# Two-layer attention and MoE kernel on one core: weaving layer-one units into left-over layer-two units, with one unit fewer in each pair of the third batch

## Chip, cores and metric

The kernel runs on one core of a Trainium2 chip. The metric is the device time of one execution in microseconds (us). Before the change four runs took 317.28, 316.82, 317.18 and 317.05 us, with a median of 317.12 us. The engines have short names below: PE is the matrix engine (TensorE), PEld its weight loads, DVE the vector engine, ACT the scalar engine, POOL the GpSimd engine and SP the engine whose queue issues most of the DMA.

## The reference

Eight batches of eight heads are computed. Each head has 512 local queries, keys and values and 32 global ones, with 64 channels. A local query attends to the 32 global keys and to the local keys at most 32 places away. A global query attends to all 544 keys. The result (8 x 544 tokens of 512 channels, 4352 rows) then passes a two-layer network with a hard-swish between the layers.

```python
s_g = scale * np.matmul(q_g, k_all.transpose(0, 1, 3, 2))
out_g = np.matmul(sm(s_g), v_all)
mask = np.abs(pos[:, None] - pos[None, :]) <= window      # window = 32
s_ll = np.where(mask, s_ll, -1000000000.0)
a_l = sm(np.concatenate([s_lg, s_ll], axis=-1))
out_l = np.matmul(a_l, np.concatenate([v_g, v_l], axis=2))
x = concat(out_g, out_l).transpose(0, 2, 1, 3).reshape(B * S, H * D)
h = x @ w_in                       # 512 -> 2048
g = h * np.clip(h + 3.0, 0.0, 6.0) / 6.0
return g @ w_out                   # 2048 -> 512
```

## The kernel before, in words

**Pairs.** The attention is cut into 32 pairs of heads, numbered p, four to a batch b = p // 4, with m = p % 4 (lines 39 to 40, NM = 4). Batches and pairs are counted from zero, so the third batch is b = 2, with pairs 8 to 11. Batches 0 and 1 are written out by hand (lines 640 to 813). Pairs 8 to 31 run in the loop at line 815.

**One pass of the loop.** For pair p the loop emits, in this order: `feed(p)` (DMA loads, POOL casts and DMA transposes for later pairs), `emit_S2(p + 1)` (scores of the next pair: 16 small matmuls into four PSUM banks, four exponentials on ACT into `E`, and four products with the window mask `mk` on DVE), `emit_SG(p + 1)` (scores of the global queries and their exponentials), `emit_AV(p)` (values: 32 small matmuls into two banks, then on DVE a reciprocal and the normalising product `xn` for each bank), `emit_PG(p)` (global queries times values) and `emit_X(p)` (transpose of `xn` into `xt`). For b < 3 and for the last pair of batch 3, `emit_X` uses PE (four transposes `psX`) and a DVE copy. For the first three pairs of batch 3 and for all later batches it is a DMA transpose on SP's queue (line 428).

**Units.** Between these parts stand four slots `M(n[0])` to `M(n[3])`. `M(n)` takes n closures from the front of the list `units` and emits them. Units are the network's work on a batch, made by `moe_units` when the batch's attention is done (line 846). There are 16 layer-one units, u1(c): four 128x512 matmuls into a bank `psH`, an ACT relu into `t`, and a DVE product into `gt{c}`. There are 16 layer-two units, u2(t, c4): four 128x512 matmuls into a bank `po`, where each group of four units (c4 = 0 to 3) ends one output tile of 128 rows, which is copied out of PSUM by DVE for even t and by ACT for odd t, and stored by a DMA. A layer-one unit thus needs ACT and DVE, and three layer-two units in four need PE alone. The number of units to a pair is set by n at line 826: 6 in batch 2, 7 in batches 3 and 4, 8 afterwards. In the list before, a batch's 16 u1 stand behind all left-over u2 of the batch in front, and its own u2 behind them.

**Left-overs.** At the end of batch 2 one u2 is left, at the end of batch 3 five, and at the end of each later batch nine.

**Order on the engines.** PE, ACT and DVE follow an order that the scheduler makes from the program. SP and POOL are pinned to program order (`pin(*QUEUES)`). All PSUM tiles but `pg` come from one pool of seven banks (`psp`, line 52); a tile whose bank was used by an earlier tile waits until that one has been read. `gt`, `xt` and `mk` are f16, and `gt` and `xt` have two buffers for each index.

**End.** After the loop two more units are emitted (line 848). Then the last 14 units (layer two of the last batch) are set aside, the units of the global tokens are put in front of them, and all is emitted.

```python
n = (1, 1, 2, 2) if b == 2 else (1, 2, 2, 2) if b in (3, 4) else (1, 2, 2, 3)
```

Of the kernel before, what the change touches and what calls it, by code (L numbers as in the profile page):

```python
# [14 lines left out]
def kernel(  # L15
# [14 lines left out]
    B, H, Sl, D = q_l.shape  # L30
# [4 lines left out]
    NC = dff // P  # L35
# [43 lines left out]
    NRUN = 2  # L79
# [90 lines left out]
    def load_g(b0, b1, nm):  # L170
        src = {"kg": k_g, "qg": q_g}[nm]
        t = stage()
        nc.sync.dma_start(
            out=t[:, 0:(b1 - b0) * HH * D].rearrange("p (n d) -> p n d", d=D),
            in_=src[b0:b1].rearrange("b (x y) s d -> (y s) (b x) d", x=HH))
        gst[b0, nm] = t

    def cast_G(b0, b1, nm, eng=nc.vector):
        n = wrk.tile([P, 4 * P], FP16, tag=nm + "n", name=nm + "n", bufs=1)
        nb = b1 - b0  # L180
        (eng.copy if eng is nc.scalar else eng.tensor_copy)(out=n[:, 0:nb * P], in_=gst[b0, nm][:, 0:nb * P])
        gst[b0, nm, "n"] = n
# [22 lines left out]
    def emit_G(b0, b1, nm):  # L205
        emit_Gp(b0, b1, nm)
        for x in range(HH):
            copy_G(b0, b1, nm, x)
# [64 lines left out]
    def wrap_q(p):  # L273
        qT = st[p]["qT"]
        last = [i for i in traced if i.engine == ET.Activation][-1]
        nc.scalar.copy(out=qT[:, 0:W], in_=qT[:, Sl:Sl + W])
        follow([i for i in traced if i.engine == ET.Activation][-1], last)

    def emit_S2(p):
        s = st[p]  # L280
        qT, kT = s["qT"], s["kT"]
        E = s["E"] = wrk.tile([P, 2, 2, Sl], FP16, tag="E", name="E", bufs=3)
        pss = [ps_tile(f"psS{i}") for i in range(4)]
        for ch in range(2):
            for w in (*range(1, NT), 0):
                c0 = w * KW if ch == 0 else ((w - 1) % NT) * KW + D
                for e in range(2):
                    r = slice(e * D, (e + 1) * D)
                    nc.tensor.matmul(out=pss[2 * ch + e][:, w * P:(w + 1) * P],  # L289
                                     lhsT=kT[r, c0:c0 + P], rhs=qT[r, w * P:(w + 1) * P])  # L290
        for ch in range(2):
            for e in range(2):
                nc.scalar.activation(out=E[:, ch, e], in_=pss[2 * ch + e], func=EXP,  # L293
                                     scale=qk_scale)
            for e in range(2):
                nc.vector.tensor_tensor(out=E[:, ch, e], in0=E[:, ch, e],  # L296
                                        in1=mk[:, ch].rearrange("p w c -> p (w c)"), op=mult)
# [43 lines left out]
    def emit_SG(p):  # L341
        b, m = divmod(p, NM)
        kT = st[p]["kT"]
        Eg = Egs[p % NE]
        ps = ps_tile("psSG")
        qz = qgz[:, m, b].rearrange("p e s -> p (e s)")
        for u in range(NT + 1):
            c0 = u * KW if u < NT else D
            nc.tensor.matmul(out=ps[:, u * 2 * Sg:(u + 1) * 2 * Sg], lhsT=kT[:, c0:c0 + P], rhs=qz)  # L349
        nc.scalar.activation(out=Eg[:, 0:NT].rearrange("p u e s -> p (u e s)"),  # L350
                             in_=ps[:, 0:NT * 2 * Sg], func=EXP, scale=qk_scale)
        r = slice(D, D + Sg)
        nc.scalar.activation(out=Eg[r, NT].rearrange("p e s -> p (e s)"),
                             in_=ps[r, NT * 2 * Sg:(NT + 1) * 2 * Sg], func=EXP, scale=qk_scale)
        if b >= NRUN:
            sum_E(p)

    xts = {}
# [62 lines left out]
    def emit_den(b):  # L421
        nc.tensor.matmul(out=pgs[b][:, 1].rearrange("p m e s -> p (m e s)"), lhsT=ones,
                         rhs=Ess[b].rearrange("p m e s -> p (m e s)"), skip_group_check=True)
# [18 lines left out]
    def emit_XG(b):  # L442
        pg = pgs[b]
        Lg = wrk.tile([P, NM, Sg], FP32, tag="Lg", name="Lg", bufs=1)
        Rg = wrk.tile([P, NM, Sg], FP32, tag="Rg", name="Rg", bufs=1)
        for e in range(2):
            r = slice(e * D, (e + 1) * D)
            nc.scalar.activation(out=Lg[r], in_=pg[r, 1, :, e], func=LN)
        nc.scalar.activation(out=Rg, in_=Lg, func=EXP, scale=-1.0)
        for e in range(2):  # L450
            r = slice(e * D, (e + 1) * D)
            nc.vector.tensor_tensor(out=xg[r, :, b], in0=Rg[r], in1=pg[r, 0, :, e], op=mult)
# [59 lines left out]
    units = []  # L512

    def M(n):
        for _ in range(n):
            if units:
                units.pop(0)()

    def local_dests(b):
        d = []  # L520
        for t in range(NT):
            row = b * S + Sg
            if t == 0:
                d.append([(W, P - W, row), (0, W, row + Sl - W)])
            else:
                d.append([(0, P, row + t * P - W)])
        return d
# [233 lines left out]
    def feed(p):  # L761
        b, m = divmod(p, NM)
        if p == 15:
            kglob(4, nc.vector)
        if m == 1 and b + 1 < B and b != 3:
            kglob(b + 1, nc.gpsimd)
        if p + 4 < NPAIR:
            if m == 0:
                vglob(b + 1, nc.gpsimd)
                vgsum(b + 1, nc.gpsimd)  # L770
            cast(p + 4, "kqv", nc.gpsimd)
            vshift(p + 4, nc.gpsimd)
        if m == 2 and b + 2 < B:
            load_vg(b + 2)
        if 2 * NM <= p + 3 < NPAIR:
            emit_TD(p + 3)
        if p + 5 < NPAIR:
            load(p + 5)
# [36 lines left out]
    for p in range(2 * NM, NPAIR):  # L815
        b, m = divmod(p, NM)
        feed(p)
        if p == 10:
            load_g(4, B, "kg")
            load_g(4, B, "qg")  # L820
        if p == 12:
            cast_G(4, B, "kg", nc.gpsimd)
            cast_G(4, B, "qg", nc.gpsimd)
        if p == 14:
            emit_G(4, B, "kg")
        n = (1, 1, 2, 2) if b == 2 else (1, 2, 2, 2) if b in (3, 4) else (1, 2, 2, 3)
        M(n[0])
        if m == 0 and b > NRUN:
            emit_den(b - 1)
            emit_XG(b - 1)  # L830
        if p + 1 < NPAIR:
            emit_S2(p + 1)
        M(n[1])
        if p + 1 < NPAIR:
            emit_SG(p + 1)
        if p + 2 < NPAIR:
            wrap_q(p + 2)
        M(n[2])
        emit_AV(p)
        emit_PG(p)  # L840
        M(n[3])
        if p == 14:
            emit_G(4, B, "qg")
        emit_X(p)
        if m == NM - 1:
            units += moe_units(lambda mm, b=b: xts[b][mm], Sl, local_dests(b), last=(b == B - 1))
        pin(*QUEUES)
    M(2)
    emit_den(B - 1)
# [39 lines left out]
```

## Time and profile before

| | |
|---|---|
| median of four runs | 317.12 us |
| profiled execution, its own time | 317.28 us |
| span from first to last instruction in it | 315.5 us |
| PE busy | 305.1 us |
| DVE, ACT, POOL busy | 212.4, 201.7, 150.7 us |
| TensorE clock granted | 1.000 |

The page of the profile gives busy times, shares of the span and instruction counts, and then the span in 40 slices, where a digit is the busy share in tenths. Two groups of matmuls carry most of the time. A row names the line, the engine, the operation, the tile written and those read, the count, the busy time with the mean of one in ns, and the idle time of the engine ahead of these instructions.

```profile
L485 PE MATMUL po<-wout,gt 128*128 128x512 f16 x528 | 122.6, 379 | 0.0
L464 PE MATMUL psH<-xt,win 128*128 128x512 f16 x512 | 119.4, 379 | 2.1 <-DVE gt L476 1.6
```

A row of a timeline has the start in us from the span's start, the length from the first start to the last end of the merged instructions, the engine, the line, the tiles, and in brackets the idle time ahead with what ended it.

### The profile page before, as it was taken

To read this page: it belongs to the slowest core of one execution; us is meant where nothing else is said; L and a number is where in the kernel's file an instruction comes from. 1 tells how busy PE (TensorE), PEld (TensorE's weight loads), DVE (VectorE), ACT (ScalarE), POOL (GpSimd) and SP (SyncE) were. 2 spreads that over 40 slices of the span, in tenths; PEclk is the share of its full clock that TensorE was granted. 3 is DMA by queue.
4 is the path that set the end of the run, shared out by engine and by line. 5 is a ranking of instruction groups with operands and counts; after the bars stand their busy time and mean duration, and the time that the engine had idled before them with its cause. 6 is when DMAs were issued, how large, how long until landed. Compare 5 with 4: busy or idle time off the path is not lost.

```text
span 315.5 us, 7303 instructions
## 1 busy us (share of the span) xinstructions
PE 305.1 (97%) x2704; PEld 162.7 (52%) x2704; DVE 212.4 (67%) x478; ACT 201.7 (64%) x418; POOL 150.7 (48%) x274
## 2 busy tenths in 40 slices
PE   7888999999999999999999999999999999999995
PEld 5454554545555455555555554555555554448444
DVE  5765878897665999579945895468743972479101
ACT  6878676896445984479844993589556941579000
POOL 4889795498766746773676458533411000000000
PEclk9999999999999999999999999999999999999999
DMA  7999999999999899799998998988632002100131
GB/s 218 245 250 250 217 190 165 206 200 173 242 208 233 193 180 175 150 230 177 173 158 192 208 177 176 173 194 162 103 98 85 18 19 83 66 2 1 40 95 68
DMA packets 140260, 48.85 MB, mean 155 GB/s; under 512 B 127552, under 2 KB 136000, under 8 KB 140224
## 3 DMA queue, kind: packets, MB, share of 16 engines
q1 hardware_dynamic: 133440, 43.93, 69.0%
q0 software_dynamic: 6784, 4.46, 10.9%
q8 instruction: 21, 0.34, 0.5%
q14 instruction: 15, 0.12, 0.1%
HBM read 35.13 MB, written 8.91 MB: 140 GB/s over the span
## 4 chain that ended last, share of the span: by engine, by line
PE 79%; DVE 7%; DMA 4%; ACT 4%; issue 2%; POOL 2%; SPq 1%; POOLq 0%
PE po L485 36%; PE psH L464 30%; PE psS L289 3%; DVE gt L476 3%; DMA win<-in_moe_w_in_dram 3%; PE pav L375 2%; PE pav L378 2%; DMA stg<-in_q_l_dram 2%; ACT t L472 1%; DVE E L296 1%; DVE xn L383 1%; PE psSG L349 1%; PE po L497 1%; PE pg L415 1%; ACT E L293 1%
## 5 line engine op out<-in xcount | busy, mean ns | idle before, releaser
L485 PE MATMUL po<-wout,gt 128*128 128x512 f16 x528 | 122.6, 379 | 0.0
L464 PE MATMUL psH<-xt,win 128*128 128x512 f16 x512 | 119.4, 379 | 2.1 <-DVE gt L476 1.6
L476 DVE SCALAR_TENSOR_TENSOR gt<-t,psH 128x512 f16<-128x512 f32 (+1 forms) x144 | 90.0, 652 | 21.1 <-ACT t L472 19.8
L472 ACT ACTIVATE t<-psH,half_col 128x512 f32<-128x512 f32 (+1 forms) x144 | 92.1, 669 | 18.4 <-PE psH L464 16.8
L464 PEld LDWEIGHTS <-win 128*128 128x128 f16 x576 | 53.3, 98 | 53.6 <-issue 1.5
L485 PEld LDWEIGHTS <-gt 128*128 128x128 f16 x528 | 48.4, 98 | 52.2
L296 DVE TENSOR_TENSOR E<-E,mk 128x512 f16<-128x512 f16 x96 | 51.8, 576 | 30.5 <-ACT E L293 29.2
L293 ACT ACTIVATE E<-psS 128x512 f16<-128x512 f32 x96 | 49.8, 604 | 13.8 <-PE psS L289 13.7
L489 ACT COPY ot<-po 128x512 f32<-128x512 f32 x16 | 9.4, 586 | 58.7 <-PE po L485 46.2
L140 POOL CAST kn<-stg 128x512 f16<-128x512 f32 x31 | 19.4, 625 | 36.4 <-DMA stg<-in_k_l_dram 35.9
L401 POOL TENSOR_TENSOR s<-Eg 128x128 f32<-128x128 f16 x24 | 10.7, 444 | 35.4 <-ACT Eg L350 34.6
L489 DVE COPY ot<-po 128x512 f32<-128x512 f32 x17 | 11.7, 690 | 22.6 <-PE po L485 22.1
L383 DVE TENSOR_TENSOR xn<-pav,rc 128x256 f16<-128x256 f32 x64 | 26.1, 421 | 1.3
L140 POOL CAST qn<-stg 128x512 f16<-128x512 f32 x31 | 20.3, 656 | 11.7 <-DMA stg<-in_q_l_dram 11.7
L140 POOL CAST vt<-stg 128x512 f16<-128x512 f32 x32 | 21.2, 663 | 8.9 <-DMA stg<-in_v_l_dram 8.3
L144 POOL COPY vb<-vt 64x512 f16<-64x512 f16 x32 | 20.6, 642 | 2.1
L378 PE MATMUL pav<-vb,E 128*128 128x65 f16 x256 | 19.9, 195 | 0.8 <-DVE vb L223 0.8
L375 PE MATMUL pav<-vt,E 128*128 128x65 f16 x256 | 20.2, 194 | 0.0
L375 PEld LDWEIGHTS <-E 128*128 128x128 f16 x256 | 17.8, 99 | 4.3 <-issue 0.8
L327 ACT ACTIVATE E<-psS 128x512 f16<-128x512 f32 x32 | 16.8, 601 | 4.0 <-PE psS L318 4.0
L378 PEld LDWEIGHTS <-E 128*128 128x128 f16 x256 | 16.9, 97 | 3.0
L289 PEld LDWEIGHTS <-kT 64*128 64x128 f16 x384 | 10.8, 94 | 9.8 <-issue 8.6
(94 smaller groups left out, 272.8 us busy)
## 6 DMA issues: line engine op xcount, KB each, us to landing
stg<-in_k_l_dram SPq DMA_DIRECT2D x32, 256.0 KB, 3.5
stg<-in_q_l_dram SPq DMA_DIRECT2D x32, 256.0 KB, 4.2
stg<-in_v_l_dram SPq DMA_DIRECT2D x32, 256.0 KB, 4.8
out_dram<-ot SPq DMA_DIRECT2D x23, 256.0 KB, 3.9
win<-in_moe_w_in_dram POOLq DMA_DIRECT2D x16, 128.0 KB, 6.6
wout<-in_moe_w_out_dram POOLq DMA_DIRECT2D x16, 128.0 KB, 4.5
out_dram<-ot SPq DMA_DIRECT2D x8, 192.0 KB, 3.1
out_dram<-ot SPq DMA_DIRECT2D x16, 64.0 KB, 2.0
```

What stands on the lines that cost most here:

```text
L140: eng.tensor_copy(out=o, in_=s[c + "f"])
L144: eng.tensor_copy(out=vbs[b % NV][0:D, :, m, vc], in_=vts[b % NV][D:P, :, m, vc])
L293: nc.scalar.activation(out=E[:, ch, e], in_=pss[2 * ch + e], func=EXP, scale=qk_scale)
L296: nc.vector.tensor_tensor(out=E[:, ch, e], in0=E[:, ch, e], in1=mk[:, ch].rearrange("p w c -> p (w c)"), op=mult)
L375: nc.tensor.matmul(out=o, lhsT=E[:, 0, e, w * P:(w + 1) * P], rhs=vt[:, w, m, c], start=True, stop=False, skip_group_check=True)
L378: nc.tensor.matmul(out=o, lhsT=E[:, 1, e, w * P:(w + 1) * P], rhs=vb[:, (w - 1) % NT, m, c], start=False, stop=True, skip_group_check=True)
L383: nc.vector.tensor_tensor(out=xn[:, 2 * w2:2 * w2 + 2].rearrange("p w (e d) -> p w e d", e=2), in0=po[:, :, 1:1 + P].rearrange("p w (e d) ...
L464: nc.tensor.matmul(out=ps[:, 0:n], lhsT=w_in_t[m][:, c * P:(c + 1) * P], rhs=rhs(m), start=(m == 0), stop=(m == NM - 1), skip_group_check= ...
L472: nc.scalar.activation(out=ts[c][:, 0:n], in_=ph[c][:, 0:n], func=RELU, bias=half_col, scale=1.0 / 6.0)
L476: nc.vector.scalar_tensor_tensor(out=gts[c][:, 0:n], in0=ts[c][:, 0:n], scalar=1.0, in1=ph[c][:, 0:n], op0=amin, op1=mult)
L485: nc.tensor.matmul(out=po[t][:, 0:dm], lhsT=gts[c][:, t * P:(t + 1) * P], rhs=w_out_t[c // 4][:, c % 4], start=(c == 0), stop=(c == NC - 1))
L489: (nc.scalar.copy if t % 2 else nc.vector.tensor_copy)(out=ot, in_=po[t][:, 0:dm])
```

## The change

A new function `weave` takes the place of `units += ...` at the end of each batch in the loop. It splits the new batch's list into its 16 u1 and the rest, and empties `units`. The left-over units are cut into a front part of `len(left) % 4` units (four more where `wait` is true, which is for b > 2) and quads of four, so a quad is one whole output tile. The front part goes first. Then the 16 u1 are dealt into one group more than there are quads, and groups and quads alternate, beginning with a group. The rest, the batch's own u2, follows. The second edit lowers the third slot of the pairs of batch 2 from two units to one.

```diff
+    def weave(new, wait):
+        u1s, rest = new[:NC], new[NC:]
+        left, out_ = units[:], []
+        del units[:]
+        h = len(left) % 4 + (4 if wait else 0)
+        out_ += left[:h]
+        quads = [left[i:i + 4] for i in range(h, len(left), 4)]
+        k = len(quads) + 1
+        for g in range(k):
+            out_ += u1s[NC * g // k:NC * (g + 1) // k]
+            if g < len(quads):
+                out_ += quads[g]
+        units.extend(out_ + rest)
...
-        n = (1, 1, 2, 2) if b == 2 else (1, 2, 2, 2) if b in (3, 4) else (1, 2, 2, 3)
+        n = (1, 1, 1, 2) if b == 2 else (1, 2, 2, 2) if b in (3, 4) else (1, 2, 2, 3)
...
         if m == NM - 1:
-            units += moe_units(lambda mm, b=b: xts[b][mm], Sl, local_dests(b), last=(b == B - 1))
+            weave(moe_units(lambda mm, b=b: xts[b][mm], Sl, local_dests(b), last=(b == B - 1)),
+                  b > NRUN)
```

The lists that follow from it: at the end of batch 2 five units are left (one and a quad), so its u1 come as eight, a quad, eight. At the end of batch 3 nine are left: five go first, and then eight u1, a quad, eight u1. At the end of batches 4 to 7 thirteen are left: five go first, and then five u1, a quad, five u1, a quad, six u1.

## The prediction

> **What bounds the kernel now.** I read the page's first two parts, then the waits of TensorE (PE) alone from 50 us on, then the engines' busy time by stretch, and last the timelines of PE, VectorE (DVE) and GpSimd (POOL) where the first two pointed.
>
> ```profile
> PE 305.1 (97%) x2704; PEld 162.7 (52%) x2704; DVE 212.4 (67%) x478; ACT 201.7 (64%) x418; POOL 150.7 (48%) x274
> PE   7888999999999999999999999999999999999995
> ```
> ```profile
> PE psH L464 <- DVE gt L476: 1.2, 4, 0.4
> ```
>
> PE is the bound, and after the head it waits for one thing only: a PSUM bank for a layer-one unit that DVE's `gt` product has not yet emptied. The starts of its matmuls tell more than these waits. In a full stream two 128x512 matmuls start 0.216 us apart (101.50 to 103.24 for eight), so a unit of four takes 0.865 us.
>
> ```profile
> 100.95 0.62 PE L289 MATMUL psS<-qT,kT 64*128 64x128 f16 x16
> 101.50 1.90 PE L464 MATMUL psH<-xt,win 128*128 128x512 f16 x8
> ...
> 106.32 2.75 PE L464 MATMUL psH<-xt,win 128*128 128x512 f16 x12 [0.41 <-DVE gt L476]
> 109.01 0.62 PE L289 MATMUL psS<-qT,kT 64*128 64x128 f16 x16
> 109.78 1.89 PE L464 MATMUL psH<-xt,win 128*128 128x512 f16 x8 [0.15 <-DVE gt L476]
> ...
> 117.06 0.81 PE L289 MATMUL psS<-qT,kT 64*128 64x128 f16 x16
> 118.28 1.97 PE L464 MATMUL psH<-xt,win 128*128 128x512 f16 x8 [0.41 <-DVE gt L476]
> ```
>
> A score block and its successor normally start 0.55 us apart (100.95 to 101.50). By such distances the starts lost are: 0.57 before 106.32 (the matmul ahead started at 105.72 and takes 0.03), 0.22 at 109.78, 0.15 at 114.16, 0.67 between 117.06 and 118.28, 0.07 after it, then 0.26 at 149.09 and 0.15 at 153.47. That is 2.1 us, all of it in the pairs of batches three and four (batches are counted from zero, and stretches named by the batch whose attention runs), and nothing after 154 us. This is the whole stock that the weave can win. The engines behind it:
>
> ```profile
> 100.00:120.00 20.00, 19.03 (x174) 9.77 (x172) 17.45 (x38) 17.65 (x37) 11.35 (x20) 1.00 0.95 187
> 120.00:138.00 18.00, 18.00 (x181) 9.74 (x179) 13.56 (x33) 9.10 (x24) 12.31 (x20) 1.00 0.86 170
> ```
>
> The columns after the length are PE, weight loads, DVE, ACT, POOL. With layer-one units in every slot DVE and ACT are 87% and 88% busy; with layer-two units ACT falls to 51%.
>
> **What the Trainium skill says.** "Perfetto Trace Analysis", Identifying the Most-Contended Engine, calls matmul busy time a bad measure because matmuls are pipelined. The trace agrees: one lasts 379 ns in the table of groups yet the next starts 216 ns later, so I count starts. "TensorE: Matmul & The Clock Gate", Wait — 56ns, not 53.3ns?, gives 215.7 ns for 512 columns warm, so nothing but waits can be won here. "SBUF — State Buffer", SBUF: two separate sides, says that a DVE operation with two SBUF inputs and a GpSimd operation lock each other out of a shared port pair for a whole instruction. The mask product `E*mk` has two such inputs, and its tile's view gives it 426 ns at the median and 1228 ns at most. The Optimization Strategy section of the first page suggests interleaving regimes with different bounds, which is what the weave does.
>
> **The change, part by part.** No operation is added or removed: 528 + 512 large matmuls stay, so the time can move only by PE's waits. The instruction order is the same up to the batch-two pairs (some 75 us).
>
> *Five units per pair in batch two.* One 0.865 us unit goes from between the score block S2(p+1) and the value block AV(p), four times, 3.46 us of work moved later and not saved. What it covered is the chain S2, ACT's exponentials, DVE's masks, reciprocals and normalised `xn`, PE's transposes psX, which stand behind two more units after AV.
>
> ```profile
> 74.60 3.47 DVE L296 TENSOR_TENSOR E<-E,mk 128x512 f16<-128x512 f16 x4 [1.57 <-ACT E L293]
> ...
> 78.75 0.42 DVE L383 TENSOR_TENSOR xn<-pav,rc 128x256 f16<-128x256 f32 x1
> ...
> 81.38 2.44 DVE L296 TENSOR_TENSOR E<-E,mk 128x512 f16<-128x512 f16 x4 [1.27 <-ACT E L293]
> ```
> ```profile
> 73.38 0.62 PE L289 MATMUL psS<-qT,kT 64*128 64x128 f16 x16
> ...
> 79.04 0.47 PE L436 MATMUL psX<-ident,xn 128*128 128x128 f16 x4
> ```
> ```profile
> 73.67 1.88 POOL L147 COPY vb<-vg 32x2048 f16<-32x2048 f16 x1
> ```
>
> S2 to psX is 5.66 us in each of the four pairs (73.38 to 79.04, 80.31 to 85.97). It becomes 4.80; the second half of `xn` is wanted 0.11 later, at 4.91.
> - Pair 8: the masks run beside POOL's copy of the global values and take 3.47 instead of 2.4. They end 4.69 after S2, and `xn` at 79.17, 5.79 after it. psX already waits (0.47; those of the next pairs take 0.39). S2 starts at the same time in both kernels, so psX ends at the same time too: the whole 0.86 is lost.
> - Pairs 9 and 11: masks end 3.51 and 3.47 after S2, normalising takes 1.1 more, `xn` is there at 4.6. Margin 0.3: no loss, 0.3 each if POOL sits less well.
> - Pair 10: in the changed order the output copy `ot` (0.6 of DVE's time, the queue moves on that fast) stands between the masks and the reciprocals. 3.67 + 0.6 + 0.9 to 1.1 is 5.2 to 5.4: loss 0.25 to 0.5, and I take 0.3.
>
> Sum 1.15, between 0.9 (pair 8 alone) and 2.1. Banks for AV are no problem: it takes those of the first two scores, read 1.6 us after S2, and comes at 2.5. The key and query transposes on SP's queue land over 7 us ahead of their scores (issued 80.85, used from 94.0), and scores come about 2.4 us sooner; no loss. POOL stands idle for its loads in these pairs, and PE's sum of exponentials waits on POOL's results with a pair in hand.
>
> *The weave in batch three* (batch two's u1 run there). `left` is 5 units at that end, h is 1, so there is one quad and the sequence is u2, eight u1, four u2, eight u1. The first eight u1 are those of before, in the same slots: six in pair 12, two in pair 13. The waits at 106.32 and 109.78 (0.79) are these, so the weave does not reach them. What differs is that slot p12.0 now ends output tile 2, copied by DVE in idle time, instead of tile 3, copied by ACT (0.59) just ahead of the logarithms. DVE's `xg` and masks end 0.5 sooner, so the fifth unit finds its bank. But the eighth wants the fifth's bank, whose `gt` stands behind relus after ACT's 2 us of exponentials and both `xn`: about 8.5 after S2, wanted at 8.1. I leave 0.45 there, between 0.2 and 0.8. Then the quad gives DVE 3.5 us with no product, and the 0.15 + 0.67 + 0.07 go. The second eight meet the `kgT` copies (four, 0.28 each) in pair 14: 0.1, between 0 and 0.3.
>
> *The weave from batch four on.* `wait` adds four u2, so `left` 9 gives h = 5, and 13 gives 5 again. The first new u1 comes in slot p16.3, where it stood already; in batches five to seven it comes five units earlier than before. It needs the last `xt`, a DMA transpose that lands 2.4 to 5.6 us after issue by its tile's view. From `xn` to its use lie five to eight units and one score block, over 6 us: no loss. The 0.26 and 0.15 belong to the eleventh and fifteenth unit of a run of sixteen, which is now cut in two: 0.05 left, at most 0.2. From batch five on there was no wait and there is nothing to win. The end of the kernel keeps its order (global tokens, then the last batch's layer two); only the 16 u1 ahead of it are spread.
>
> Sum: 2.1 lost before; after 1.15 + 0.45 + 0.1 + 0.05 = 1.75. Gain 0.35 us. The profiled execution took 317.28 us with a span of 315.5 (1.8 outside it), and stands 0.16 above the median; 317.12 - 0.35 is 316.8.
>
> **The rivals.**
> - *Nearly even* (forecast), 316.8, own range 316.2 to 317.3: the stalls in batch three and those made in batch two pay each other.
> - *The weave wins*: the head of batch three loses only its low end 0.2, pair 10 fits, pair 8 loses 0.86. 2.1 - 1.1 is 1.0: 316.1. For it: DVE starts batch three 0.5 sooner. Against: in pair 13 the bank waits for a product late in DVE's queue.
> - *Slower: the short pairs bind on the mask chain.* Place: psX in pairs 9 to 11. Price: if POOL collides there as in pair 8, masks end 4.69 after S2, `xn` 5.8, and psX loses 0.9 each; 0.86 + 2.7 + 0.6 against 2.1 is 2.1 slower, 319.2; half of it gives 318. It decides when the three lose over 0.5 each, which is masks ending 4.2 after S2. Against: those pairs showed 3.5 to 3.7, though POOL was casting then too.
> - *Loads fall behind*: scores in batch three wait for their transposes; 7 us of margin must go first. About 318.
> - *The change does not act where it means to* is true of the first eight units of both batches and is in the forecast.
>
> **How the numbers follow.** Nearly even 0.52, weave wins 0.27, mask chain 0.16, loads 0.05. A measurement here tells 0.2% (0.63 us) from no change. Of the forecast's own spread 0.09 lies beyond that on the fast side and 0.01 on the slow one. Faster 0.27 + 0.09 = 0.36, slower 0.16 + 0.05 + 0.01 = 0.22, within 0.42. The low end 315.9 takes in the weave's win with pair 14 and batch four at zero; the high end 318.0 takes half the mask case. Outside lie less than 2 in 10.
>
> **What would show it.** psX of pair 8 should wait about 0.9 us for `xn` and end within 0.1 us of 79.4; psX of pair 10 about 0.3; none in pairs 9 and 11. At S2 of pair 13's scores PE should be 2.0 to 2.4 us ahead of before, with 3.46 us of work still owed. One wait for `gt` should remain near the eighth u1 of batch three and none from there to the end. I am wrong if psX waits in all four pairs, if several `gt` waits remain after the quad, or if u1 waits for `xt`.

## The result and the profile after

| | before | after |
|---|---|---|
| median | 317.09 us (54 runs) | 318.42 us (34 runs) |
| lowest and highest | 315.66, 319.21 us | 316.13, 319.99 us |
| profiled execution, its own time | 317.28 us | 317.56 us |
| span of it | 315.5 us | 315.8 us |

The ratio after to before is 1.0039, with a 95% interval from 1.0028 to 1.005, so the changed kernel is slower by 0.39%. The medians stand 1.33 us apart, the means 1.24 us. Four executions in a slower state, three of the kernel before (324 us and more) and one of the version in the last row of the experiments' table (320.31 us), are left out of medians and ratios. The forecast was 316.8 us in a range of 315.9 to 318.0, so the measured median lies above the range. One profiled execution shows less than the medians do, 0.28 us, because it is one draw from a wide spread. For this reason six executions of the changed kernel and two of the old one were traced in all.

The first rows of the page after, and the waits of PE from 50 us on:

```profile
PE 305.3 (97%) x2704; PEld 162.9 (52%) x2704; DVE 220.0 (70%) x478; ACT 202.6 (64%) x418; POOL 151.6 (48%) x274
PE   8898999998999999999999999999999999999995
```
```profile
PE psX L436 <- DVE xn L383: 1.3, 2, 1.1
PE psH L464 <- DVE gt L476: 0.7, 1, 0.7
```

PE is as busy as it was, but DVE grew from 212.4 to 220.0 us with the same 478 instructions, so its instructions took longer each (212.4 and 214.0 us in two traces before, 217.1 to 220.0 in six after). PE now waits for two things instead of one. The first is new: the transposes of pair 8 wait for the normalised values. Here are both on PE's timeline after, with the score blocks of pairs 9, 11, 13, 14 and 16 around them:

```profile
72.75 0.62 PE L289 MATMUL psS<-qT,kT 64*128 64x128 f16 x16
...
78.79 0.28 PE L436 MATMUL psX<-ident,xn 128*128 128x128 f16 x2 [1.08 <-DVE xn L383]
79.33 0.28 PE L436 MATMUL psX<-ident,xn 128*128 128x128 f16 x2 [0.26 <-DVE xn L383]
...
85.21 0.39 PE L436 MATMUL psX<-ident,xn 128*128 128x128 f16 x4
...
86.39 0.62 PE L289 MATMUL psS<-qT,kT 64*128 64x128 f16 x16
...
91.19 0.39 PE L436 MATMUL psX<-ident,xn 128*128 128x128 f16 x4
...
97.17 0.39 PE L436 MATMUL psX<-ident,xn 128*128 128x128 f16 x4
...
98.46 0.62 PE L289 MATMUL psS<-qT,kT 64*128 64x128 f16 x16
...
104.12 2.75 PE L464 MATMUL psH<-xt,win 128*128 128x512 f16 x12 [0.70 <-DVE gt L476]
106.81 0.62 PE L289 MATMUL psS<-qT,kT 64*128 64x128 f16 x16
107.46 1.02 PE L464 MATMUL psH<-xt,win 128*128 128x512 f16 x4
...
122.33 0.93 PE L289 MATMUL psS<-qT,kT 64*128 64x128 f16 x16
```

From the scores to the transposes there are now 4.80 us (86.39 to 91.19), as computed. Pairs 9 to 11 don't wait. Pair 13's scores start at 98.46, 2.49 us ahead of before; pair 8 began 0.63 us sooner in this execution, and in the mean of six the lead is 2.25 us, within the 2.0 to 2.4 of the forecast. The first score block in the fence, at 72.75, leads to a wait of 1.08 us and one of 0.26 in pair 8. Batch three begins with one wait for `gt`, at 104.12, and has no more. The block at 122.33 takes 0.93 where it should take 0.62: its second half starts late.

On DVE's timeline after, the rows behind these waits are the mask products of pairs 9 to 13 (as scores are made one pair ahead, the product at 73.97 belongs to pair 9 and stands ahead of the normalising of pair 8):

```profile
73.97 4.21 DVE L296 TENSOR_TENSOR E<-E,mk 128x512 f16<-128x512 f16 x4 [1.33 <-ACT E L293]
...
81.47 2.26 DVE L296 TENSOR_TENSOR E<-E,mk 128x512 f16<-128x512 f16 x4 [1.27 <-ACT E L293]
...
87.45 2.04 DVE L296 TENSOR_TENSOR E<-E,mk 128x512 f16<-128x512 f16 x4 [1.39 <-ACT E L293]
...
93.43 2.15 DVE L296 TENSOR_TENSOR E<-E,mk 128x512 f16<-128x512 f16 x4 [1.40 <-ACT E L293]
...
100.11 3.24 DVE L296 TENSOR_TENSOR E<-E,mk 128x512 f16<-128x512 f16 x4
103.38 1.88 DVE L476 SCALAR_TENSOR_TENSOR gt<-t,psH 128x512 f16<-128x512 f32 x3
```

And POOL's timeline after, where the global values of the next batch are copied once in four pairs:

```profile
73.77 1.89 POOL L147 COPY vb<-vg 32x2048 f16<-32x2048 f16 x1
...
99.77 1.89 POOL L147 COPY vb<-vg 32x2048 f16<-32x2048 f16 x1
```

Four masks take 2.0 to 2.3 us, except twice: 4.21 and 3.24 us. Both times the copy lies upon them. The second meeting is new. Here are POOL's and DVE's timelines before at that place (two views):

```profile
98.60 1.88 POOL L147 COPY vb<-vg 32x2048 f16<-32x2048 f16 x1
```
```profile
102.68 0.43 DVE L296 TENSOR_TENSOR E<-E,mk 128x512 f16<-128x512 f16 x1 [2.17 <-ACT E L293]
...
103.63 1.92 DVE L296 TENSOR_TENSOR E<-E,mk 128x512 f16<-128x512 f16 x3
```

The copy ran from 98.60 to 100.48 and the masks began at 102.68. After the change the masks begin at 100.11, because PE is 2.5 us ahead, while the copy ends at 101.66: POOL waits for its loads, and its copy even came 1.2 us later.

The tile view of `E` after, between 72 and 82 us, gives shortest, median and longest ns of its mask products:

```profile
L296 DVE TENSOR_TENSOR E<-E,mk x6: 814/825/1965, 71.8 to 81.5; 128x512 f16<-128x512 f16 x6
```

The longest is 1965 ns, where the kernel before had 1228 at most. Beside the 0.43 us that a product took at the median before, it was held for 1.5 us, which is most of the 1.69 us for which the copy still ran when the masks began. The link holds in all twenty traces of the study: from 66 us on they have 1940 mask products, 36 of which took over 1.0 us, and the copy lay upon each of the 36; the longest of the others took 0.88 us.

By stretch (the columns are length, PE, weight loads, DVE, ACT, POOL, clock, DMA share, GB/s):

```profile
100.00:120.00 20.00, 19.27 (x186) 10.30 (x184) 17.86 (x39) 16.47 (x36) 12.10 (x20) 1.00 1.09 195
120.00:138.00 18.00, 17.90 (x162) 9.20 (x161) 14.32 (x34) 10.11 (x23) 12.57 (x21) 1.00 1.04 186
```

In the first stretch, which now holds work that stood some 2.5 us later before, PE gained 0.24 us, and ACT is eased, 16.47 us for 17.65, as the weave spreads the layer-one units; DVE is not, 17.86 for 17.45.

**Bookkeeping.** From pair 8's scores to the last matmul, the time less the late matmul starts is 240.1 to 240.3 us in the traces of both kernels. So the late starts and the time at which pair 8 begins account for an execution. They add up as follows, in us. The mean of six executions of the changed kernel is over traces with times from 317.18 to 319.40 us; the two before took 317.28 and 317.2. The count takes nothing off where the matmuls behind a wait start closer together than usual, so it runs some 0.1 us high where a score block is interrupted, and up to 0.4 us in a whole trace.

| late starts at | before (two traces) | after (this trace) | after (mean of six) | prediction |
|---|---|---|---|---|
| transposes of pair 8 | 0.08, 0.49 | 1.66 | 1.40 (1.15 to 1.78) | 0.86 more than before |
| transposes of pairs 9 to 11 | 0 | 0 | 0.03 | 0.3 |
| first eight layer-one units of batch three | 0.80, 0.86 | 0.97 | 1.32 (0.68 to 2.68) | 0.45 |
| rest of batch three, to pair 16's scores | 0.89, 0.89 | 0.31 | 0.31 | 0.1 |
| batch four | 0.39, 0.24 | 0.09 | under 0.1 | 0.05 |
| all, with those too small to list | 2.28, 2.64 | 3.19 | 3.28 | 1.75 |

Pair 8 begins at 68.97 us in the mean of six and at 68.91 in the mean of two, so nothing is lost ahead of it. The mean of the times is 318.08 against 317.24, which is 0.84 more; that of the late starts 3.28 against 2.46, which is 0.82 more. The traces thus explain 0.84 us of the 1.33 between the medians (1.24 between the means); six draws from a spread of 4 us leave room for the rest.

### The profile page after: what moved, and what is told of

The parts are those of the page before. It is cut to its first block, busy times and chain, and to the rows that moved or that the text cites. A ratio compares the mean times of both kernels' runs of the same rounds, so it can differ in the third digit from the quotient of the medians.

```text
span 315.8 us, 7301 instructions
## 1 busy us (share of the span) xinstructions
PE 305.3 (97%) x2704; PEld 162.9 (52%) x2704; DVE 220.0 (70%) x478; ACT 202.6 (64%) x418; POOL 151.6 (48%) x274
## 4 chain that ended last, share of the span: by engine, by line
PE 86%; DVE 9%; ACT 3%; issue 1%; ACTq 0%
PE po L485 35%; PE psH L464 33%; PE psS L289 4%; DVE E L296 2%; PE pav L375 2%; PE pav L378 2%; DVE gt L476 2%; DVE xn L383 2%; PE psSG L349 1%; PE psS L302 1%; PE psS L318 1%; PE warm L570 1%; PE po L497 1%; PE pg L415 1%; ACT E L327 1%
## 5 line engine op out<-in xcount | busy, mean ns | idle before, releaser
L485 PE MATMUL po<-wout,gt 128*128 128x512 f16 x528 | 124.2, 379 | 0.0
L476 DVE SCALAR_TENSOR_TENSOR gt<-t,psH 128x512 f16<-128x512 f32 (+1 forms) x144 | 91.9, 655 | 37.1 <-ACT t L472 35.8
L472 ACT ACTIVATE t<-psH,half_col 128x512 f32<-128x512 f32 (+1 forms) x144 | 93.1, 670 | 34.8 <-PE psH L464 33.7
L296 DVE TENSOR_TENSOR E<-E,mk 128x512 f16<-128x512 f16 x96 | 55.2, 617 | 9.1 <-ACT E L293 7.9
```

The lines of the kernel that those rows point to most:

```text
L296: nc.vector.tensor_tensor(out=E[:, ch, e], in0=E[:, ch, e], in1=mk[:, ch].rearrange("p w c -> p (w c)"), op=mult)
L472: nc.scalar.activation(out=ts[c][:, 0:n], in_=ph[c][:, 0:n], func=RELU, bias=half_col, scale=1.0 / 6.0)
L476: nc.vector.scalar_tensor_tensor(out=gts[c][:, 0:n], in0=ts[c][:, 0:n], scalar=1.0, in1=ph[c][:, 0:n], op0=amin, op1=mult)
L485: nc.tensor.matmul(out=po[t][:, 0:dm], lhsT=gts[c][:, t * P:(t + 1) * P], rhs=w_out_t[c // 4][:, c % 4], start=(c == 0), stop=(c == NC - 1))
```

## The experiments

Ratios are against the kernel before on the same chip, with 95% intervals; a ratio need not be the quotient of the medians (1.0034 for the version with the unit kept in pairs 9 to 11, whose median is 0.19% above that of before). "Late starts" are counted in the one trace of each kernel, from pair 8 on.

| kernel | median, us (runs) | ratio, interval | traced time; late starts |
|---|---|---|---|
| changed, copy moved behind the casts | 318.38 (22) | 1.0033, 1.0017 to 1.0049 | 316.03; 1.19. Second trace 319.47; 4.10 |
| before, copy moved likewise | 317.26 (14) | 1.0012, 0.9995 to 1.0029 | 316.82; 2.55 |
| changed, fifth unit kept ahead of the values | 317.27 (14) | 1.0006, 0.9989 to 1.0023 | 317.50; 1.97 |
| before, five units per pair, no weave | 317.71 (22) | 1.0019, 1.0004 to 1.0033 | 318.44; 2.85 |
| changed, no copy in the loop | 317.43 (22) | 1.0013, 0.9999 to 1.0027 | 316.94; 2.42 |
| before, no copy in the loop | 316.77 (14) | 0.9987, 0.9968 to 1.0007 | 317.09; 1.35 |
| unit kept and copy moved | 317.76 (22) | 1.0014, 0.9996 to 1.0032 | 317.74; 2.21 |
| unit kept and copy cut in four | 317.89 (22) | 1.0037, 1.0016 to 1.0057 | 319.76; 5.40 |
| unit kept in pair 8 alone | 318.04 (14) | 1.0029, 1.0006 to 1.0052 | 317.41; 1.48 |
| unit kept in pairs 9 to 11 alone | 317.80 (22) | 1.0034, 1.0016 to 1.0051 | 317.39; 2.63 |
| unit kept, five layer-two units first | 316.98 (21) | 1.0005, 0.9985 to 1.0025 | 316.17; 1.44 |

### The copy moved behind the casts

The edit moves the copy of the global values (`vglob`), and the shorter second copy of them (`vgsum`, which despite its name makes no sums), behind the casts in POOL's program order, in the changed kernel and, as a control, in the kernel before.

```diff
         if p + 4 < NPAIR:
+            cast(p + 4, "kqv", nc.gpsimd)
+            vshift(p + 4, nc.gpsimd)
             if m == 0:
                 vglob(b + 1, nc.gpsimd)
                 vgsum(b + 1, nc.gpsimd)
-            cast(p + 4, "kqv", nc.gpsimd)
-            vshift(p + 4, nc.gpsimd)
```

> The changed kernel with one edit: POOL copies the global values of the next batch behind the four casts and shifts of a batch's first pair instead of ahead of them; every other engine keeps its order. Theory A (the loss is the meeting of this 1.9 us copy with the mask products): the four masks of pair 8 fall from 4.2 to about 2.3 us, the psX wait of pair 8 from 1.6 to at most 0.2, the gt wait at the head of batch three from 0.9 to about 0.4, and the time by 1.5 to 2 us, to 0.998 of before or less. Theory B (the short pairs alone, whatever POOL does): psX of pair 8 still waits about 0.9 and the time stays within 0.3 us of the changed kernel.

> The kernel of before with the same move of POOL's copy as in the run named late. In before the copy lies on pair 8's masks (3.5 us) but six units hide them, and it ends ahead of batch three's masks. Theory A expects a change under 0.3 us either way: psX of pair 8 loses its 0.08, the gt waits of batches three and four stay at about 2 us. A theory that POOL's copy costs time in itself expects a gain of 1 us here too.

The median did not move: 318.38 against 318.42. The trace, with 316.03 us the shortest of any changed kernel, looked as if the cure had worked. Its tile view of `E` in the same stretch:

```profile
L296 DVE TENSOR_TENSOR E<-E,mk x10: 410/474/801, 71.6 to 81.9; 128x512 f16<-128x512 f16 x10
```

With the copy at 77.80, no product took over 801 ns, pair 8 did not wait, and the late starts came to 1.19. As trace and median contradicted each other, the same kernel was traced again.

> The kernel of the run named late again (POOL's copy behind the casts). Its profiled execution took 316.03, the shortest of its 22, and lost only 1.2 us from pair 8 on, with a median of 318.38. Theory C expects psX waits in pairs 9 to 11 where this execution is longer than 317.5; theory D psH waits for xt in batches five to seven; theory E a later start of pair 8's scores than 69.1 us.

This time 319.47 us. POOL's copy came at 81.47, on the masks of the pair behind. DVE's and PE's timelines of that trace:

```profile
75.10 1.89 DVE L296 TENSOR_TENSOR E<-E,mk 128x512 f16<-128x512 f16 x4 [1.70 <-ACT E L293]
80.92 4.11 DVE L296 TENSOR_TENSOR E<-E,mk 128x512 f16<-128x512 f16 x4 [1.02 <-ACT E L293]
```
```profile
85.65 0.28 PE L436 MATMUL psX<-ident,xn 128*128 128x128 f16 x2 [0.82 <-DVE xn L383]
86.19 0.28 PE L436 MATMUL psX<-ident,xn 128*128 128x128 f16 x2 [0.26 <-DVE xn L383]
```

The wait of pair 8 has become one of pair 9: 1.41 us of late starts. So for the transposes the mechanism stands: masks without the copy take 1.9 to 2.0 us and masks with it 4.1, and in none of the twenty traces do the transposes `psX` lose over 0.1 us without it. Batch three lost 2.47 more, and about 2.0 of that has another cause: its first eight layer-one units were late between 107 and 110 us, although the masks of pair 13 took 1.89 us, with no copy near them (it came at 110.12). What they waited for is shown further down, where the changed kernel is traced again. The theory that a later copy would win 1.5 to 2 us falls: POOL's order fixes only what the copy stands behind, and its time varies by 3.7 us between two executions of one kernel. In the kernel before, the move changed nothing that the interval tells from zero.

### The fifth unit kept between scores and values

The change takes a unit out of the third slot, ahead of the values. Here the five units per pair stay, but the empty slot is the first one, ahead of the next pair's scores.

```diff
-        n = (1, 1, 1, 2) if b == 2 else (1, 2, 2, 2) if b in (3, 4) else (1, 2, 2, 3)
+        n = (0, 1, 2, 2) if b == 2 else (1, 2, 2, 2) if b in (3, 4) else (1, 2, 2, 3)
```

> The changed kernel with the missing unit of batch two's pairs taken ahead of the scores (0, 1, 2, 2) and not between scores and values. The score block and the transposes stand 5.66 us apart again. Theories A and B both expect the psX wait of pair 8 to go (0.5 at most where the masks still meet POOL's copy, since they then end about 4.8 us after the scores) and a gain of 1.1 to 1.6 us over the changed kernel. Theory A expects the gt wait at the head of batch three to stay at 0.6 to 1.0; a theory that the loss sits in the weave itself expects no gain.

The scores to the transposes are 5.66 us again, pair 8 loses 0.39 in the trace, and the median is 317.27, 1.15 us below the changed kernel and level with before. Everything else of the change, the weave and the number of units, is the same. So the place from which the unit is taken costs about 1.1 us, most of the loss; by the two intervals it can be anything from 0.2 to 2 us.

### The short pairs without the weave

```diff
-        n = (1, 1, 2, 2) if b == 2 else (1, 2, 2, 2) if b in (3, 4) else (1, 2, 2, 3)
+        n = (1, 1, 1, 2) if b == 2 else (1, 2, 2, 2) if b in (3, 4) else (1, 2, 2, 3)
```

This is the only edit, made in the kernel before.

> The kernel of before with five units per pair in batch two and no weave; five layer-two units then stand ahead of batch two's layer-one units. If the short pairs make the loss, the psX wait of pair 8 is 0.9 to 1.6 us, and about four gt waits come back in batches three and four (1 to 2 us), so that it is 1 to 2 us slower than before. If the weave makes the loss, it is within 0.3 us of before.

The loss is 0.19% (0.6 us, less than the 1 to 2 us expected), half of the whole change's, with 1.41 us late at pair 8. The weave on top of it did not win its 1.3 us. Batch three's first rows on PE's timeline tell why:

```profile
99.40 0.62 PE L289 MATMUL psS<-qT,kT 64*128 64x128 f16 x16
99.95 1.90 PE L485 MATMUL po<-wout,gt 128*128 128x512 f16 x8
101.84 1.89 PE L485 MATMUL po<-wout,gt 128*128 128x512 f16 x8
104.20 2.75 PE L464 MATMUL psH<-xt,win 128*128 128x512 f16 x12
```

Without the weave, all five left-over layer-two units come first. They need no bank that waits for DVE, so the masks beside the copy (3.54 us at 101.06) hurt nobody, and no start is late at 104.20. The weave puts only one of the five first and eight layer-one units behind it, right under the slow masks. Later on it takes away 1.32 us (0.34, 0.67, 0.07 and 0.24 here) and leaves 0.4; at the start it adds the 1.32 that the six traces show in the mean. By these traces, then, the weave on top of the short pairs loses 0.4 us rather than winning; between the medians it is 0.7.

### The changed kernel traced again

Five more traces of the changed kernel and one more of the kernel before, with no edit.

> The changed kernel again, for one more trace: its 34 runs lie between 316.1 and 320.0 us, and the one profiled so far (317.56) is one of the shorter. Counting lost starts of matmuls from pair 8's scores on, that one lost 3.2 us of 243.5 and the rest, 240.3, is the same in all traces so far to 0.2. Theory C: executions of 318.4 and more lose 4 us or more, as psX waits for xn also in pairs 9 to 11, where the masks meet POOL's casts. Theory D: they lose it in batches five to seven, where the first layer-one units wait for a DMA transpose. Theory E: they lose it ahead of pair 8, where both kernels have the same order.

> As for again1: a further trace of the changed kernel, to see where a longer execution loses its starts. Theories C, D and E as there.

> The changed kernel, a fourth trace. Theory F: in executions over 318.5 the gaps at the head of batch three come so close together that the granted clock falls to a half for some 3 us behind them, as in the trace of the run named slot0_split (0.52 from 107.5 to 111), which adds 1 to 2 us. Theory C (psX in pairs 9 to 11 too) and E (a later start of pair 8) as before.

> The changed kernel, a fifth trace; theories F, C and E as for again3.

> The changed kernel, a sixth trace. The five so far lost 2.7 to 3.2 us from pair 8 on and took 317.2 to 318.6. If it takes over 319, theory F expects a stretch with the granted clock below 0.8, theory C a psX wait in pairs 9 to 11, theory E a start of pair 8's scores later than 70 us.

> The kernel of before again, for a second trace beside its first (2.3 us of lost starts from pair 8's scores on, at 69.1 us): the sum of its lost starts should be 2.0 to 2.6 us again, and the head of batch three 0.6 to 1.0 of it.

They took 318.35, 317.18, 318.64, 317.33 and 319.40 us, and 317.2 for the kernel before. Pair 8 waits in all five, and pairs 9 to 11 lose 0.09 at most, in the short and in the long ones: theory C, that the spread comes from there, falls. Theory D falls as well, as nothing is lost in batches five to seven. That the loss comes from ahead of pair 8 (E) falls too, by the equal means above, although pair 8 begins anywhere from 68.24 to 69.86 us. What differs between executions is, first, how late POOL's copy is. By its second start, at 98.89, 99.58, 99.77, 100.90, 101.09 and 101.49 us in the six, the first units of batch three lost 0.68, 0.90, 0.97, 1.42, 1.27 and 2.68. In the first of these, which is the shortest execution, the masks took 2.28 us; in the last, the longest, 3.43, and PE's timeline there has four waits:

```profile
104.55 2.75 PE L464 MATMUL psH<-xt,win 128*128 128x512 f16 x12 [0.90 <-DVE gt L476]
107.83 0.56 PE L289 MATMUL psS<-qT,kT 64*128 64x128 f16 x8 [0.36 <-DVE gt L476]
108.71 0.39 PE L289 MATMUL psS<-qT,kT 64*128 64x128 f16 x7 [0.32 <-DVE xn L383]
109.30 1.02 PE L464 MATMUL psH<-xt,win 128*128 128x512 f16 x4 [0.19 <-DVE gt L476]
```

That is 2.68 us of late starts. The granted clock was 1.000, so a fall of it (theory F) isn't needed for a long execution.

The masks explain only the first of the four waits: in two other traces they took longer (3.68 and 3.54 us) and half as much was lost. A second thing differs: when the queries of pair 14 arrive. Behind `emit_SG`, each pass of the loop also calls `wrap_q(p + 2)`, in which ACT copies a piece of the transposed queries `qT` of pair p + 2. So ACT needs that DMA transpose about 3 us before PE needs it for the scores (106.00 and 109.01 for pair 14 before). While ACT waits, the relus `t` behind this copy wait too, and with them the products `gt`, which give PE its banks back. These rows are from ACT's timelines before, after and in the longest trace, and from DVE's in the longest:

```profile
106.00 0.22 ACT L276 COPY qT<-qT 128x32 f16<-128x32 f16 x1
```
```profile
103.24 0.22 ACT L276 COPY qT<-qT 128x32 f16<-128x32 f16 x1
```
```profile
105.46 0.22 ACT L276 COPY qT<-qT 128x32 f16<-128x32 f16 x1 [2.01 <-DMA qT<-qn]
```
```profile
106.42 0.69 DVE L476 SCALAR_TENSOR_TENSOR gt<-t,psH 128x512 f16<-128x512 f32 x1 [1.32 <-ACT t L472]
```

Before, the transpose landed at 100.27 us, 5.7 ahead of ACT's copy. In the profile after it landed at 103.07, 0.17 ahead: the copy came 2.8 us sooner, while the transpose was issued 0.9 us later and took 4.4 us instead of 2.5. In the longest trace it landed at 105.43, and ACT stood idle for 2.01 us. Six traces of versions with layer-one units at the head of batch three separate the two causes, as no mask product of pair 13 took over 0.9 us in them. Their late starts, in us, are counted here by whole distances, without the 0.1 that an interrupted score block adds:

| trace | ACT's wait for the queries | first eight layer-one units late by |
|---|---|---|
| copy moved, first trace | 0 | 0.58 |
| changed, 317.18 us | 0 | 0.58 |
| changed, no copy | 0.56 | 1.12 |
| unit kept and copy moved | 0.72 | 1.28 |
| copy moved, second trace | 1.42 | 1.99 |
| unit kept, copy cut in four | 2.03 | 2.64 |

So in these traces ACT's wait is passed on in full. In the trace of the short pairs without the weave ACT waited 1.51 us and PE lost nothing there, as layer-two units stood in its place. ACT waits over 0.5 us here in seven of the sixteen traces with five units per pair, and in none of the four with six. No run moves this copy or the transpose, so what the wait costs in the medians isn't measured.

### Without the copy

The call of the copy is taken out of the loop, in both kernels; which part of the values that leaves out stands in the expectation.

```diff
             if m == 0:
-                vglob(b + 1, nc.gpsimd)
                 vgsum(b + 1, nc.gpsimd)
```

> The changed kernel without POOL's copy of the global values in the loop: batches three to seven keep the global values of an earlier batch in their value tile, so that part of their local outputs is left out. If the meeting of that copy with the mask products is the loss, psX of pair 8 waits 0.2 us or less, lost starts from pair 8 on fall from 3 to about 1 us in the median, and the time to 316.0 to 316.6 us, ratio 0.997 to 0.999, with fewer runs above 318. If the copy is not the cause, the ratio stays at 1.003 to 1.004.

> The kernel of before without that copy (the same part left out). Its pairs of six units hide the copy in batch two, but the gt waits of batches three and four are made by the layer-one units: expected is a gain of 0 to 0.4 us over before, so less than half of what the changed kernel gains from the same cut, and lost starts near 2 us.

The changed kernel gains, from 1.0039 to 1.0013, though less than expected (317.43 us, where 316.0 to 316.6 stood in the expectation). The old one goes from 1 to 0.9987, which its interval doesn't tell from nothing. In the changed kernel's trace no `psX` waits; 1.23 us remain at the head of batch three, where ACT waits 0.56 us for the queries, and a layer-one unit at 165.41 us is 0.56 late, waiting for the DMA transpose of `xt`, as in no other trace. The copy is worth 0.26% (0.8 us) after and 0.13% (0.4 us) before, by ratios whose intervals are 0.2% to 0.4% wide. So it explains a part of the loss, about 0.4 us of it by these values, and not all.

### Combinations

Three versions build on the kept unit: the copy moved, the copy cut into four pieces behind the casts of four pairs, and all five left-over layer-two units put ahead of the layer-one units of batch two.

```diff
             if m == 0:
-                vglob(b + 1, nc.gpsimd)
                 vgsum(b + 1, nc.gpsimd)
             cast(p + 4, "kqv", nc.gpsimd)
             vshift(p + 4, nc.gpsimd)
+            nc.gpsimd.tensor_copy(
+                out=vbs[(b + 1) % NV][rg, :, m, vc],
+                in_=vg[rg, b + 1].rearrange("s (m h) d -> s m (h d)", h=2)[:, m].unsqueeze(1)
+                .to_broadcast([Sg, NT, P]))
...
-                  b > NRUN)
+                  b >= NRUN)
```

> The changed kernel with both edits: the missing unit taken ahead of the scores, and POOL's copy behind the casts. If the two causes add, it is 0.5 to 1 us faster than the kernel with slot 0 alone (317.27), 316.5 or so, ratio 0.998. If the copy's place matters little in the median, as the run named late suggests, it is equal to slot 0 within 0.3 us.

> A full kernel: the changed one with the missing unit taken ahead of the scores (0, 1, 2, 2), and POOL's 1.9 us copy cut into four of about 0.6 us, one behind the casts of each pair. If the meeting of a long copy with the masks is what remains of the loss (0.4 at psX of pair 8, about 1.0 at the head of batch three), lost starts fall from 2.0 to about 1.0 us and the time to 316.2 to 316.6, ratio 0.997 to 0.999. If short POOL work collides as much as one long copy, it stays at 317.3.

> A full kernel: the run named slot0, with all five left-over layer-two units of batch one put ahead of batch two's layer-one units, so that these begin in slot 3 of pair 12, behind the logarithms and the first masks. If the weave of batch two loses because its first six units stand in pair 12 with the logarithms and the global products, the waits near the head of batch three fall from about 1.0 to 0.4 us, a wait of 0.7 comes back near the last units (no quad is left to cut the run of sixteen), batch four keeps its gain, and the time is 316.6 to 317.1, ratio 0.998 to 1.000. If not, it is equal to slot0 or slower.

Moving the copy adds nothing to the kept unit (317.76 against 317.27, intervals overlapping). Cutting it is no better in the median (317.89), although its pieces took only 0.6 to 0.8 us each and no mask product of pairs 9 to 13 took over 0.9 us: in its trace ACT waited 2.03 us for the queries. Putting the layer-two units first did what it should in its trace, the shortest but one of the study. The wait at the head of batch three is gone, although the copy lay on the masks (3.45 us) and ACT waited 1.21 us for the queries:

```profile
101.92 2.75 PE L464 MATMUL psH<-xt,win 128*128 128x512 f16 x12
...
113.67 1.97 PE L464 MATMUL psH<-xt,win 128*128 128x512 f16 x8 [0.41 <-DVE gt L476]
```

Of its 1.44 us of late starts 0.87 lie in the run of sixteen layer-one units, which this order has again, and 0.45 in batch four. Its median, 316.98, is that of the kernel before on the same chip (317.04). No version of the study is clearly faster than before: this one and the kept unit are level with it.

### Which of the short pairs

The unit is kept in pair 8 alone, or in pairs 9 to 11 alone, with the weave.

```diff
+        n = (0, 1, 2, 2) if p == 8 else (1, 1, 1, 2) if b == 2 else (1, 2, 2, 2) if b in (3, 4) else (1, 2, 2, 3)
```
```diff
+        n = (1, 1, 1, 2) if p == 8 else (0, 1, 2, 2) if b == 2 else (1, 2, 2, 2) if b in (3, 4) else (1, 2, 2, 3)
```

> The changed kernel with slots (0, 1, 2, 2) in pair 8 alone; pairs 9 to 11 keep (1, 1, 1, 2). If psX of pair 8 is the place where the short pairs lose, it equals the run named slot0 (1.0006) within 0.3 us, about 1 us faster than the changed kernel. If pairs 9 to 11 lose as well in longer executions, it stays at 1.002 to 1.004.

> The complement of the run named pair8: pair 8 keeps (1, 1, 1, 2) and pairs 9 to 11 have (0, 1, 2, 2). If psX of pair 8 is the one place of the loss, it equals the changed kernel, ratio 1.003 to 1.004, with 1.2 to 1.8 us lost at psX of pair 8. If the short pairs 9 to 11 share it in executions that the traces miss, as the 1.0029 of pair8 suggests, it lies about half way between slot0 and the changed kernel, 1.001 to 1.003.

In the traces the matter is plain: with the unit kept in pair 8 its late starts are 0.39, with it taken there they are 1.41, and pairs 9 to 11 lose nothing in either. In the ratios it is not. A short pair 8 alone gives 1.0034, nearly the whole loss; but keeping the unit in pair 8 alone gives 1.0029, and not the 1.0006 of keeping it in all four. Both intervals hold 1.002 to 1.005, and that of the second reaches down to 1.0006. How much of the loss the pairs 9 to 11 carry stays open.

## Why the prediction was wrong

**Right.** The operations, the distance of 4.80 us, and the claim that time moves only by PE's waits hold. Pair 8 waits, and pairs 9 and 11 don't. In no trace of the changed kernel does PE wait for a transpose of keys or queries, or for `xt`. The weave takes away the late starts of the second part of batch three and those of batch four, down to 0.31 and under 0.1 us. None of the three signs that were to show the forecast wrong came: the loss lay in sizes and places that they did not cover.

**Wrong, pair 8.** "They end 4.69 after S2, and `xn` at 79.17" took the masks' 3.47 us from one execution as if it were their length. It was not: that copy had begun 0.93 us before the masks and had 0.95 us left, and the longest product took 1.23. In the profile after, the copy starts 0.20 us before them, one product takes 1.97, and the masks end 5.43 after S2 (72.75 to 78.18). Pair 8 loses 1.40 us in the mean where 0.86 was added to an old loss that was near nothing: 0.5 too little. The page of the Trainium skill "SBUF — State Buffer", SBUF: two separate sides, on which the step rested, says that whoever comes second waits for the whole instruction; a product held for 1.5 us of the copy's remaining 1.69 agrees, to 0.2 us. The bound to take from it was the copy's full length, and it stood in the text without being used.

**Wrong, the head of batch three.** "DVE's `xg` and masks end 0.5 sooner, so the fifth unit finds its bank", and 0.45 us left of 0.79. The masks took 3.24 us instead of 2.35 (0.43 + 1.92 before), and 1.32 us are lost in the mean. The step moved PE and DVE forward by the units that were taken out, and left out that POOL's copy would not move with them: it ended 2.2 us ahead of the masks before, and lies on them after. This is the larger of the two, 0.87 us, but not all of it is the copy's. By an estimate from the traces it has three parts. About 0.1 us is lost beyond the forecast where neither copy nor wait is at work (0.58 for 0.45). About 0.2 comes from the wait for the queries in the longest trace, which lost some 1.2 us more than two others with masks as long, spread over six. The rest, about 0.5, comes from the copy.

**Wrong, the query transposes.** "The key and query transposes on SP's queue land over 7 us ahead of their scores" is right for pair 14 before (100.27 and 109.01), but the first to need the queries is ACT, in `wrap_q`, 3 us sooner. The 5.7 us that were left there shrank to 0.17 in the profile after, and ACT waited 0.20, 0.25 and 2.01 us in three of the six traces. The step set this at "no loss"; what it cost is within the 0.87 above. The rival that loads fall behind had a late transpose right and the place wrong, the scores; it was given 0.05.

**Wrong, small.** Pair 10 was to lose 0.3 and lost nothing, since its masks took 2.04; pair 16's scores lose 0.3, where 0.1 was left for the stretch.

These terms, 0.54 + 0.87 - 0.3 + 0.2, make up 1.3 of the 1.5 us between 1.75 and 3.28; the rest are starts late by under 0.05. The rival that the short pairs bind on the mask chain had the mechanism, an operation of POOL upon the masks, and a fair price (318 for half of it). It had the place wrong: not pairs 9 to 11, but pair 8 and the start of batch three. It was given 0.16, because the margins of pairs 9 to 11, which do hold, were read as speaking against it as a whole.

**Open.** The traces of six executions explain 0.84 of 1.33 us. Whether longer executions, in the tail up to 319.99, lose in other places or wait oftener for the queries is not known; nor is the share of pairs 9 to 11.

## What to carry to other kernels

When work on one engine is moved ahead, list the long operations of engines that are paced by something else, here POOL by its loads, and ask what they will now lie upon: they don't come along. Do the same for every reader of a transfer, not only for the last one: here the scores had 7 us to spare, while ACT's copy of the same queries ran out of its margin. A chain that runs beside such an operation is to be priced with its full length and not with the overlap that one execution shows. And where a kernel's executions spread by 4 us, one trace is one draw: the shortest trace of a changed kernel here, 316.03 us, came from a version with a median of 318.38.

## What was not expected of the hardware

In the trace of the kept unit with the copy cut in four (319.76 us), TensorE's granted clock fell in the middle of the kernel. Its busy times by stretch; the columns are PE, weight loads, DVE, ACT, POOL, and then the clock:

```profile
100.00:104.00 4.00, 4.00 (x38) 2.12 (x37) 1.93 (x4) 1.95 (x6) 1.05 (x2) 1.00 1.12 97
104.00:107.50 3.50, 1.78 (x19) 0.89 (x18) 2.67 (x7) 3.48 (x8) 1.26 (x3) 1.00 1.29 244
107.50:111.00 3.50, 3.32 (x8) 1.14 (x9) 3.50 (x7) 2.21 (x5) 3.33 (x5) 0.52 1.21 215
111.00:115.00 4.00, 4.00 (x42) 2.25 (x41) 2.11 (x6) 1.19 (x4) 3.74 (x9) 0.99 1.09 230
```

In 3.5 us PE was busy for only 1.78, waiting four times for `gt` and `xn` behind ACT's 2.03 us wait for the queries, and the 3.5 us after that ran at 0.52 of the clock: eight matmuls, each 0.21 us late, 1.7 us in all beside the 2.65 us of waits. The page of the Trainium skill "TensorE: Matmul & The Clock Gate", Part 1: The HAM clock gate (the "warmup" mystery), names half the clock after an idle window of about 3.4 us. The half clock agrees; but here PE was half busy by its records, and its longest wait was 0.93 us. By starts it had less to do: in the 3.2 us up to 107.68 only one score block started, 0.55 us of work (an estimate from its distance in a full stream). So a cluster of short waits can cost more than their sum. Two other traces had such a cluster and kept the clock at 1.00: the longest of the changed kernel and the second of the moved copy, with 2.2 and 2.6 us around the one score block, estimated likewise. Where the limit lies, and whether other executions lose their clock, is not shown.
